# Attention, routing and two MLP layers on one core: another order for ScalarE's copies and the router's exp and ln

## The chip, the cores and the metric

The kernel runs on one core of a Trainium2 chip. A core has five engines that run their own instruction streams in order and meet at semaphores: TensorE (PE in the profile; PEld is its weight load), VectorE (DVE), ScalarE (ACT), GpSimd (POOL) and SyncE (SP). The metric is the device time of one execution in microseconds; less is better.

## The reference

`q`, `k`, `v` have 4 batches, 8 heads, 768 steps and a head width of 48; the token rows of width 384 go through two layers after the attention.

```python
k_n = k / (norm(k) + 1e-06)
for t in range(S):                                   # attention, a delta rule
    y[t]   = einsum('bhd,bhde->bhe', q[t], state)
    v_old  = einsum('bhde,bhd->bhe', state, k_n[t])
    state += beta[t] * einsum('bhd,bhe->bhde', k_n[t], v[t] - v_old)
x = y as 3072 x 384
noisy = x @ w_gate + log1p(exp(x @ w_noise)) * noise # routing, 8 experts, the best 2 of each token
out   = sum over the two of weight * (relu(x @ w1[e]) @ w2[e])
h     = out @ w_in                                   # second layer
final = (h * clip(h + 3, 0, 6) / 6) @ w_out
```

## The kernel before

The tokens are cut into 24 tiles of 128 rows (64 steps of two batches). A tile's delta rule is solved in blocks: Gram products of its rows, the inverse of a triangular matrix, and products with the state. Four tiles make a group. The loop of the attention takes two tiles, n and n+1, in each turn, for n = 0, 2, ..., 18; a turn whose n is a multiple of four is called a four turn here. The last four tiles are written out behind the loop.

The names that follow:

- `gram(a)` and `gram(a + 1)`, with a = n + 8, multiply the keys and queries of the tiles eight ahead (line 183) and put the copies of the result into a list `late`; `flush(k)` issues the first k copies of it, `flush()` all. The copies run on ScalarE: m0 and m1 fill `mq` (L187), o fills the off-diagonal block `goff` (L205), d0, d1 and d2 fill the diagonal pieces `gd` of the group (L199, then L202 twice). `gd` has one buffer. `masked` belongs to m.
- The inverse of a group runs on VectorE. Its head transposes `gd` (L276), its large products and reductions are L342 to L356, its tail transposes the result into `Xc` (L364) and `Yc` (L365). It is queued at the end of the turns n = 2, 6, 10 and 14 for the groups 2 to 5, and issued piece by piece as a credit that grows with TensorE's work allows (`run`).
- `merge1(n)` multiplies `goff` with `Xc` on TensorE (L389) and ScalarE copies the result to `y` (L392). `merge2(n)` multiplies `y` with `Yc` (L408), and ScalarE scales the result into `Xc` (L152, two pieces of 32 rows). `prep(n)` scales a part of `Xc` in place (L152, 128 rows). merge1(n+1) on TensorE waits for the last copy that wrote `Xc` ahead of it.
- `ks` (copied to `rz`, L431), `solve`, `update` (copied to `us`, L150) and `output` (copied to `x`, L150) are the products with the state.
- The router: `transposes` of a finished tile (L840) with the copy to `rt_xt` (L842), `logits` (L853, copied to `rt_ls`, L855). `route` gives stages for four tiles: exp on ScalarE (L880), ln on ScalarE (L883), a row of small VectorE operations (L888 and on, the noisy logits and the best two), counts, the rank on TensorE (L924 to L930, copied to `rt_rks` by ScalarE, L932; VectorE reads it into `rt_pos`, L934) and the moves of rows. One call of `step()` issues one stage; what it holds for VectorE is woven into the inverse's operations.
- `warm(m)` issues m matmuls of a zero tile on TensorE (L480).

The order of the instructions on each engine is that in which this code is written, except that VectorE's operations come out of the list `pend` by credit. Behind the attention the two layers follow, with TensorE busy nearly all the time.

Of the kernel before, what the change touches and what calls it, by code (L numbers as in the profile page):

```python
# [27 lines left out]
PQ = 1.3  # L28
P2 = 3
P3 = 1  # L30
P4 = 26
F = [0, 0, 2, 1, 0, 0, 0, 0]
FG = [2, 0, 1, 0, 0, 0, 0, 1]
FL = [1, 3, 3, 3, 1, 1, 0, 3]
# [9 lines left out]
KD = DM // 128  # L44
# [45 lines left out]
def emit_attention(ctx, tc, qk, k, v, beta, const, rt, moe):  # L90
# [77 lines left out]
    def load_beta(g):  # L168
        t = wk.tile([128, 32], F32, tag="beta", name="beta")
        nc.sync.dma_start(out=t, in_=beta[g])  # L170
        beta_t[g] = t

    def gram_tiles(n):
        g, j = divmod(n, 4)
        if j == 0:
            gd[g] = pr.tile([128, 32, 32], F32, tag="gd", name="gd", bufs=1)
        goff[n] = wk.tile([128, NH, 32], F32, tag="goff", name="goff", bufs=11)

    def products(n, gm, heads, lo, hi):
        for i, h in enumerate(heads):  # L180
            for b in range(2):
                m = mq[b][n % NM][st[b], :, h]
                nc.tensor.matmul(gm[tok[b], i, lo:hi], lhsT=m[:, 1, :], rhs=m[:, lo // 64:hi // 64, :],
                                 start=True, stop=True)

    def evict_m(n, gm, hs, b):
        nc.scalar.copy(out=mq[b][n % NM][tok[b], 0, hs, :], in_=gm[tok[b], :, 0:64])  # L187

    def masked(n):
        if n < 6:  # L190
            masks.append(n)
        else:
            mask(n)

    def evict_d(n, gm, hs, part):
        g, j = divmod(n, 4)
        d = gd[g][:, 8 * j + hs.start:8 * j + hs.stop, :]
        if part == 0:
            nc.scalar.copy(out=d, in_=gm[:, :, 64:96])  # L199
        else:  # L200
            p = slice(64 * part - 32, 64 * part)
            nc.scalar.copy(out=d[p], in_=gm[p, :, 96:128])  # L202

    def evict_o(n, gm, hs):
        nc.scalar.copy(out=goff[n][:, hs, :], in_=gm[:, :, 64:96])  # L205
# [25 lines left out]
    def gram(n):  # L231
        gram_tiles(n)
        gm = ps1.tile([128, NH, 128], F32, tag="gm", name="gm")
        hs = slice(0, NH)
        products(n, gm, range(NH), 0, 128)
        late.extend(lambda b=b: evict_m(n, gm, hs, b) for b in range(2))
        late.append(lambda: (masked(n), evict_o(n, gm, hs)))
        late.extend(lambda part=part: evict_d(n, gm, hs, part) for part in range(3))

    masks = []  # L240

    def mask(n):
        for b in range(2):
            m = mq[b][n % NM][tok[b], 0]
            nc.gpsimd.affine_select(out=m, in_=m, pattern=[[0, NH], [1, CH]], compare_op=ALU.is_gt,
                                    fill=0.0, base=0, channel_multiplier=-1)
# [133 lines left out]
    y1, xs = {}, {}  # L380
# [94 lines left out]
    def warm(m):  # L475
        if not m:
            return
        p = ps2.tile([128, 512], F32, tag="tp", name="wp")
        for _ in range(m):
            nc.tensor.matmul(p, lhsT=wz[:, 0:128], rhs=wz, start=True, stop=True)  # L480

    pend, late = [], []

    def flush(k=99):
        for _ in range(min(k, len(late))):
            late.pop(0)()
# [5 lines left out]
    def weave(ops, k=1):  # L492
        micro[0] += len(ops)

        def one(fn):
            fn()
            micro[0] -= 1

        ops = [(0.1, lambda fn=fn: one(fn)) for fn in ops]
        steps, last = pend[:-1], pend[-1:]  # L500
        pend[:] = []
        for it in steps:
            pend.append(it)
            pend.extend(ops[:k])
            ops = ops[k:]
        pend.extend(ops + last)

    def step(drain=False):
        if drain:
            while stages or micro[0]:  # L510
                while micro[0]:
                    pend.pop(0)[1]()
                if stages:
                    weave(stages.pop(0)() or [])
        elif stages and not micro[0]:
            weave(stages.pop(0)() or [], 2)
            run(0.0)

    def straight(k):
        for _ in range(k):  # L520
            for fn in stages.pop(0)() or []:
                fn()
# [4 lines left out]
    def run(t, drain=False):  # L527
        credit[0] = min(credit[0] + t, 4.0) if pend else 0.0
        while pend:
            c, fn = pend[0]  # L530
            if not drain and credit[0] < c:
                break
            pend.pop(0)
            credit[0] -= c
            fn()
        if drain:
            credit[0] = 0.0
# [6 lines left out]
    def live(fn, n, *args):  # L544
        if 0 <= n < NT:
            fn(n, *args)
            cur = pc[0] - LA
            if fn in beat:
                rt.beat = beat[fn](n)
                lives[0] += 1  # L550
            tok = rt.moves[0][0] if rt.moves else NT
            if tok < NT - 16 and fn in beat and lives[0] % 2 == 0 and cur >= tok // 4 * 4 + 8 or \
                    NT - 16 <= tok < NT - 12 and fn in beat and cur >= NT - 8 or \
                    NT - 12 <= tok < NT - 8 and cur >= NT - 6 and fn not in (load_v, load_k, load_qk, v_norm):
                rt.moves.pop(0)[1]()
                if tok >= NT - 12 and not rt.moves:
                    moe.snap_load()
            run((PACE if pc[0] < NT else PACE_L) * PE_US.get(fn.__name__, 0.0))
# [29 lines left out]
    for i in range(8, 16):  # L588
        n, hh = divmod(i, 2)
# [15 lines left out]
    ks(1)  # L605
    warm(P4)
    for i in range(2):
# [6 lines left out]
    for n in range(0, NT - 4, 2):  # L614
        a = n + LA
        four = n % 4 == 0
        pc[0] = a
        if not four and a // 4 + 1 < NG:
            load_beta(a // 4 + 1)
        for i in range(2):  # L620
            live(load_v, n + 4 + i)
            if n + 4 < NT:
                live(load_k, n + 2 + i)
        for i in range(2):
            if n + 2 + i > 3:
                live(v_norm, n + 2 + i)
        if n == NT - 6:
            moe.snapshot(pk, ps2)
        if n:
            warm(W0.get(n, W0[-(four + 1)]))  # L630
            live(merge1, n)
            live(prep, n)
            live(ks, n)
            rt.transposes(n - 2, xs.pop(n - 2))
            live(gram, a)
            live(prep, n + 1)
            if n != NT - 6:
                step()
            live(merge2, n)
            flush(2)  # L640
            live(ks, n + 1)
            live(merge1, n + 1)
            if n == NT - 6:
                straight(2)
            live(solve, n)
            live(merge2, n + 1)
            flush()
            rt.transposes(n - 1, xs.pop(n - 1))
            rt.logits(n - 2)
        else:  # L650
            live(solve, n)
            live(gram, a)
            flush()
        step()
        live(update, n)
        live(solve, n + 1)
        if n:
            rt.logits(n - 1)
            if four:
                step(True)  # L660
                stages += rt.route(n - 4, 4)
                if n == NT - 8:
                    straight(2)
        live(output, n)
        live(load_qk, a + 2)
        if n == NT - 8:
            straight(2)
        elif not four:
            step()
        live(gram, a + 1)  # L670
        live(update, n + 1)
        flush(2)
        live(output, n + 1)
        if n == NT - 6:
            rt.reserve()
            while rt.moves:
                rt.moves.pop(0)[1]()
                if not rt.moves:
                    moe.snap_load()
        flush()  # L680
        live(load_qk, a + 3)
        if n != NT - 8:
            step()
        if not four:
            run(0.0, True)
            if n == NT - 10:
                step()
            if n // 4 + 2 < NG:
                pend += inverse_ops(n // 4 + 2)
                run(2.3)  # L690
    step(True)
    n = NT - 4
# [76 lines left out]
class Router:  # L769
# [64 lines left out]
    def store(self, n, x):  # L834
        self.nc.sync.dma_start(out=self.xd[n * 128:(n + 1) * 128, :], in_=x)

    def transposes(self, n, x):
        tp = self.ps.tile([128, 4, 128], F32, tag="tp", name="tpx", bufs=2)
        for k in range(KD):
            self.nc.tensor.transpose(tp[:, k, :], x[:, k * 128:(k + 1) * 128], self.const["ident"])  # L840
        xt = self.wk.tile([128, KD, 128], F32, tag="rt_xt", name="rt_xt", bufs=2)
        self.nc.scalar.copy(out=xt, in_=tp[:, 0:KD, :])  # L842
        self.xt[n] = xt

    def logits(self, n):
        nc = self.nc
# [828 lines left out]
```

## Time and profile before

| | |
|---|---|
| three runs | 1187.56, 1191.43, 1191.59 us; median 1191.43 us |
| profiled execution | 1189.55 us, span 1187.8 us, mean granted clock of TensorE 0.955 |
| busy, share of the span | PE 96%, DVE 57%, ACT 43%, POOL 25% |
| 0 to 258.7 us, loop of the attention | PE busy 230.68 us, DVE 230.22, ACT 174.59; clock 0.87 |
| 258.7 to 298 us, last four tiles and routing | PE busy 32.51 us of 39.3; clock 0.67 |
| 298 to 1187.8 us, the two layers | PE busy 876.40 us of 889.8; clock 0.99 |

In the rows further down, a line of a timeline holds the start in us from the span's start, the duration in us, the engine, the kernel's line and operation, what it writes and reads, the number of instructions in a row, and in brackets the idle time before it with what ended it. A row of a table of stretches holds the busy time of each engine in the stretch.

### The profile page before, as it was taken

The numbers are of one execution on the slowest core, as the hardware profiler recorded it, in microseconds if no ns is written. First come the engines' busy times: TensorE is split into PE (matmuls) and PEld (weight loads), VectorE is DVE, ScalarE is ACT, GpSimd is POOL, SyncE is SP. The second block draws the span as 40 slices with busy tenths as digits, with TensorE's granted clock in tenths as the row PEclk, the third lists the DMA queues.
The fourth block names the chain that finished last, engine by engine and source line by source line (L and its number), as shares of the span: only waits on it lengthen the run. The fifth ranks groups of instructions, "written<-read, shape, count | busy, mean of one in ns | idle before, by whom it ended". The sixth has DMA issues, their size and how long they took to land. (4 is left out here: it accounts for less than half of the span.)

```text
span 1187.8 us, 25674 instructions
## 1 busy us (share of the span) xinstructions
PE 1139.6 (96%) x10578; PEld 1047.3 (88%) x10593; DVE 677.7 (57%) x1573; ACT 509.8 (43%) x1060; POOL 302.5 (25%) x370
## 2 busy tenths in 40 slices
PE   8899989878899999999999999999999999999998
PEld 5588878777699999999999999979989898989988
DVE  7999789885538676756565534444251614334250
ACT  5578767635514232323232324454251514334240
POOL 4542356562534223222223230132000000000000
PEclk9898977967799999999999999999999999999999
DMA  7642443424064464445343310732101020200000
GB/s 200 145 132 75 114 91 70 69 48 143 2 245 164 141 207 135 159 147 190 118 172 119 129 50 10 233 105 71 34 27 51 3 73 8 66 15 8 20 1 27
DMA packets 56220, 113.35 MB, mean 95 GB/s; under 512 B 9368, under 2 KB 37221, under 8 KB 55334
## 3 DMA queue, kind: packets, MB, share of 16 engines
q1 hardware_dynamic: 47142, 90.32, 25.5%
q0 software_dynamic: 8448, 19.70, 5.1%
q10 hardware_dynamic: 512, 1.67, 0.6%
q8 instruction: 84, 1.38, 0.5%
q14 instruction: 34, 0.28, 0.1%
HBM read 83.74 MB, written 26.08 MB: 92 GB/s over the span
## 5 line engine op out<-in xcount | busy, mean ns | idle before, releaser
L1224 PE MATMUL yp<-w2h,ht 128*128 128x384 f32 x832 | 221.2, 340 | 0.0
L1224 PE MATMUL yp<-w2l,ht 128*128 128x384 f32 x448 | 150.4, 336 | 0.0
L1224 PEld LDWEIGHTS yp<-w2h,ht 128*128 128x128 f32 x832 | 148.4, 188 | 0.3
L1014 POOL DMA_INDIRECT y<-ys,idp x56 | 64.9, 1159 | 303.2 <-DVE ys L1233 224.1
L1201 PE MATMUL hp<-xth,w1h 128*128 128x416 f32 (+2 forms) x384 | 137.9, 359 | 1.2 <-DVE xtl L1143 1.2
L1201 PE MATMUL hp<-xtl,w1h 128*128 128x416 f32 (+2 forms) x384 | 136.7, 356 | 0.0
L1201 PE MATMUL hp<-xth,w1l 128*128 128x416 f32 (+2 forms) x384 | 136.5, 355 | 0.0
L1564 PE MATMUL yp<-woh,gh 128*128 128x384 f32 x384 | 130.4, 340 | 0.0
L1564 PE MATMUL yp<-wol,gh 128*128 128x384 f32 x384 | 129.1, 336 | 0.0
L1564 PE MATMUL yp<-woh,gl 128*128 128x384 f32 x384 | 129.1, 336 | 0.0
L1204 ACT ACTIVATE ht<-hp 128x416 fp32r<-128x416 f32 (+2 forms) x128 | 66.3, 518 | 132.6 <-PE hp L1201 132.5
L1207 DVE SCALAR_TENSOR_TENSOR ht<-hp,ht 128x352 fp32r<-128x352 f32 (+3 forms) x192 | 79.3, 441 | 64.6 <-ACT ht L1204 64.2
L1532 PE MATMUL hp<-xh,wih 128*128 128x512 f32 x288 | 112.7, 391 | 2.6 <-DVE three L1518 2.6
L1532 PE MATMUL hp<-xh,wil 128*128 128x512 f32 x288 | 112.9, 392 | 0.0
L1532 PE MATMUL hp<-xl,wih 128*128 128x512 f32 x288 | 112.8, 392 | 0.0
L1541 DVE TENSOR_TENSOR gl<-r,gh 128x512 fp32r<-128x512 f32 x96 | 66.5, 693 | 79.6 <-ACT gh L1540 79.6
L1535 ACT ACTIVATE r<-hp,three 128x512 f32<-128x512 f32 x96 | 66.1, 688 | 89.7 <-PE hp L1532 87.2
L1537 DVE SCALAR_TENSOR_TENSOR r<-r,hp 128x512 f32<-128x512 f32 x96 | 65.4, 681 | 53.2 <-ACT r L1535 53.2
L1224 PEld LDWEIGHTS yp<-w2l,ht 128*128 128x128 f32 x448 | 84.1, 188 | 0.0
L1571 ACT ACTIVATE os<-yp 128x384 f32<-128x384 f32 x23 | 11.3, 491 | 152.8 <-PE yp L1564 152.8
L1201 PEld LDWEIGHTS hp<-xth,w1h 128*128 128x128 f32 x384 | 73.2, 191 | 3.9 <-DVE xtl L1143 1.6
L1201 PEld LDWEIGHTS hp<-xth,w1l 128*128 128x128 f32 x384 | 73.2, 191 | 2.1
(228 smaller groups left out, 2199.5 us busy)
## 6 DMA issues: line engine op xcount, KB each, us to landing
r<-in_moe_w_dram SPq DMA_DIRECT2D x16, 768.0 KB
r<-in_moe_w_dram SPq DMA_DIRECT2D x21, 512.0 KB
yg<-y SPq DMA_DIRECT2D x24, 384.0 KB
wd_r<-in_moe_w_in_dram SPq DMA_DIRECT2D x6, 1024.0 KB
wd_r<-in_moe_w_out_dram SPq DMA_DIRECT2D x8, 768.0 KB
mq<-in_qk_dram SPq DMA_DIRECT2D x28, 192.0 KB
v<-in_v_dram SPq DMA_DIRECT2D x24, 192.0 KB
xd<-x SPq DMA_DIRECT2D x24, 192.0 KB
```

The source lines that it names most:

```text
L1014: return nc.gpsimd.indirect_dma_start(out=y, out_offset=bass.IndirectOffsetOnAxis(ap=idx, axis=0), in_=src, in_offset=None, bounds_check=y ...
L1201: nc.tensor.matmul(p[:, 0:w], lhsT=a[:, k, fs], rhs=b[:, k, c], start=(i == 0), stop=(i == 3 * KD - 1))
L1204: nc.scalar.activation(out=h[:, c], in_=p[:, 0:w], func=ACTF.Relu)
L1207: nc.vector.scalar_tensor_tensor(out=h[:, rest(lo, hi)], in0=p[:, lo - c.start:hi - c.start], scalar=0.0, in1=h[:, lo:hi].bitcast(F32), op ...
L1224: nc.tensor.matmul(p[0:2 * m if pair else m, 0:DM], lhsT=a, rhs=b[:, f, :], start=f == i == 0, stop=f == FT - 1 and i == len(terms) - 1)
L1532: nc.tensor.matmul(p, lhsT=a[:, k, fs], rhs=b[:, k, :], start=(i == 0), stop=(i == 3 * KD - 1))
L1535: nc.scalar.activation(out=r, in_=p, func=ACTF.Relu, bias=three)
L1537: nc.vector.scalar_tensor_tensor(out=r, in0=r, scalar=6.0, in1=p, op0=ALU.min, op1=ALU.mult)
L1541: nc.vector.tensor_tensor(out=gl[:, f, :], in0=r, in1=gh[:, f, :].bitcast(F32), op=ALU.subtract)
L1564: nc.tensor.matmul(p[:, 0:DM], lhsT=a[:, f, c], rhs=b[:, f, :], start=(i == 0), stop=(i == 3 * FT2 - 1))
L1571: nc.scalar.mul(out=t, in_=p[:, 0:DM], mul=1.0 / 6.0)
```

## The change

Five things change.

1. Of the copies of a Gram the diagonal pieces d0, d1, d2 now come first, then o, then m0 and m1 with `masked`. For the first Gram of a turn one copy (d0) is issued ahead of ks(n+1) and the rest behind merge2(n+1). For the second Gram four copies (d0, d1, d2, o) are issued right behind it, ahead of `update`, and the two m copies behind `output`.
2. merge2(n) comes right behind the first Gram; its copies into `Xc` are issued ahead of the copy to `rt_xt`, which `transposes` now hands back instead of issuing it. prep(n+1) comes behind merge1(n+1).
3. The `step()` in the middle of the turn comes behind merge2(n).
4. At the end of the four turns n = 4, 8 and 12 a second `step()` follows the first: ln comes right behind exp. (The turn n = 16 has no step there.)
5. `P4`, the warming matmuls ahead of the first merge, goes from 26 to 32.

```diff
-P4 = 26
+P4 = 32
...
-        late.extend(lambda b=b: evict_m(n, gm, hs, b) for b in range(2))
-        late.append(lambda: (masked(n), evict_o(n, gm, hs)))
         late.extend(lambda part=part: evict_d(n, gm, hs, part) for part in range(3))
+        late.append(lambda: evict_o(n, gm, hs))
+        late.append(lambda: evict_m(n, gm, hs, 0))
+        late.append(lambda: (evict_m(n, gm, hs, 1), masked(n)))
...
-            rt.transposes(n - 2, xs.pop(n - 2))
+            copies = []
+            rt.transposes(n - 2, xs.pop(n - 2), copies)
             live(gram, a)
-            live(prep, n + 1)
+            live(merge2, n)
+            copies.pop()()
             if n != NT - 6:
                 step()
-            live(merge2, n)
-            flush(2)
+            flush(1)
             live(ks, n + 1)
             live(merge1, n + 1)
+            live(prep, n + 1)
...
         live(gram, a + 1)
+        flush(4)
         live(update, n + 1)
-        flush(2)
         live(output, n + 1)
...
         if n != NT - 8:
             step()
+            if n and four:
+                step()
...
-    def transposes(self, n, x):
+    def transposes(self, n, x, later=None):
...
-        self.nc.scalar.copy(out=xt, in_=tp[:, 0:KD, :])
         self.xt[n] = xt
+        copy = lambda: self.nc.scalar.copy(out=xt, in_=tp[:, 0:KD, :])
+        if later is None:
+            copy()
+        else:
+            later.append(copy)
```

ScalarE at the end of the turn n = 4, from the copies of `us` of the last update to the first merge copy of the next turn. Before:

```order
L150 COPY us_152<-sd 48x384
L150 COPY us_156<-sd 48x384
L187 COPY mq_132<-gm 64x512
L187 COPY mq_142<-gm 64x512
L150 COPY x<-y 128x384
L205 COPY goff<-gm 128x256
L199 COPY gd<-gm 128x256
L202 COPY gd<-gm 32x256 x2
L880 ACT_TABLE_LOAD
L880 ACTIVATE rt_t<-rt_ls 128x32
L392 COPY y_1963<-mg 128x256
```

and now:

```order
L199 COPY gd<-gm 128x256
L202 COPY gd<-gm 32x256 x2
L205 COPY goff<-gm 128x256
L150 COPY us_152<-sd 48x384
L150 COPY us_156<-sd 48x384
L150 COPY x<-y 128x384
L187 COPY mq_132<-gm 64x512
L187 COPY mq_142<-gm 64x512
L889 ACT_TABLE_LOAD
L889 ACTIVATE rt_t<-rt_ls 128x32
L892 ACT_TABLE_LOAD
L892 ACTIVATE rt_t<-rt_t 128x32
```

The diagonal pieces and `goff` moved ahead of `us`, the copies to `mq` behind `x`, and ln (L892 now) with its table load directly behind exp.

ScalarE at the start of the turn n = 6, up to the copies of the first Gram. Before:

```order
L392 COPY y_1963<-mg 128x256
L152 ACTIVATE Xc<-Xc,half 128x8x32
L431 ACTIVATE rz_157<-ks 128x384
L842 COPY rt_xt<-tpx 128x384
L152 ACTIVATE Xc<-Xc,half 128x8x32
L883 ACT_TABLE_LOAD
L883 ACTIVATE rt_t<-rt_t 128x32
L152 ACTIVATE Xc<-mg 32x8x32 x2
L187 COPY mq_133<-gm 64x512
L187 COPY mq_143<-gm 64x512
L431 ACTIVATE rz_158<-ks 128x384
L392 COPY y_2070<-mg 128x256
```

and now:

```order
L393 COPY y_1970<-mg 128x256
L152 ACTIVATE Xc<-Xc,half 128x8x32
L432 ACTIVATE rz_157<-ks 128x384
L152 ACTIVATE Xc<-mg 32x8x32 x2
L848 COPY rt_xt<-tpx 128x384
L199 COPY gd<-gm 128x256
L432 ACTIVATE rz_158<-ks 128x384
L393 COPY y_2076<-mg 128x256
L152 ACTIVATE Xc<-Xc,half 128x8x32
```

The two merge copies into `Xc` stood behind `rt_xt`, prep and the ln, and stand directly behind `rz` now; of the Gram's copies one stands ahead of the second `rz` instead of two.

VectorE in the second half of the inverse of group 2, where the router's first small operations are woven in. Before:

```order
L342 TENSOR_TENSOR big<-A,TT 128x256
L345 TENSOR_REDUCE tmp<-big 128x16x4 x2
L353 TENSOR_TENSOR big<-T,tmp 128x1024
L353 TENSOR_TENSOR A<-T,tmp 128x768
L888 TENSOR_SCALAR rt_t<-rt_t 128x32
L889 SCALAR_TENSOR_TENSOR rt_t<-rt_t 128x32
L356 TENSOR_REDUCE T<-big 128x4x16
```

and now:

```order
L343 TENSOR_TENSOR big<-A,TT 128x256
L897 TENSOR_SCALAR rt_t<-rt_t 128x32
L898 SCALAR_TENSOR_TENSOR rt_t<-rt_t 128x32
L346 TENSOR_REDUCE tmp<-big 128x16x4
L899 SCALAR_TENSOR_TENSOR rt_t<-rt_t 128x32
L900 RECIPROCAL rt_t<-rt_t 128x32
L346 TENSOR_REDUCE tmp<-big 128x16x4
```

The first router operation (it reads exp's result) and the second (it reads ln's) moved ahead of two reductions and two products.

## Rows read from the trace of the kernel before

**Rows 1.** Stretches: from:to us, length, busy us (xinstructions) of PE PEld DVE ACT POOL, PEclk, DMA, GB/s.
```profile
298.00:1187.80 889.80, 876.40 (x4721) 826.90 (x4721) 427.48 (x786) 317.28 (x578) 158.53 (x155) 0.99 0.28 91
```
**Rows 2.** Timeline of VectorE, 84 to 217 us: start, us, instruction, idle before.
```profile
84.23 1.99 DVE L276 STREAM_TRANSPOSE A<-gd 128x1024 f32<-128x1024 f32 x1 [1.65 <-ACT gd L202]
...
105.76 1.27 DVE L345 TENSOR_REDUCE tmp<-big 128x64 f32<-128x768 f32 x2
...
127.05 1.99 DVE L276 STREAM_TRANSPOSE A<-gd 128x1024 f32<-128x1024 f32 x1 [6.36 <-ACT gd L202]
...
149.09 0.41 DVE L342 TENSOR_TENSOR big<-A,TT 128x256 f32<-128x256 f32 x1
...
170.25 1.98 DVE L276 STREAM_TRANSPOSE A<-gd 128x1024 f32<-128x1024 f32 x1 [2.71 <-ACT gd L202]
...
216.05 0.23 DVE L934 TENSOR_TENSOR rt_pos<-rt_rks,ebase 128x32 f32<-128x32 f32 x1 [4.19 <-ACT rt_rks L932]
```
**Rows 3.** Timeline of TensorE, 44 to 260 us.
```profile
44.80 0.69 PE L389 MATMUL mg<-Xc,goff 32*32 32x32 f32 x32 [3.80 <-DVE Xc L364]
...
83.84 0.69 PE L389 MATMUL mg<-Xc,goff 32*32 32x32 f32 x32
...
95.22 0.53 PE L853 MATMUL lg<-wgn,rt_xt 128*64 128x16 f32 x12 [0.28 <-ACT rt_xt L842]
...
96.64 1.96 PE L183 MATMUL gm<-mq 64*64 64x128 f32 x32
...
100.32 0.82 PE L480 MATMUL wp<-wz 128*128 128x512 bf16 x2
101.07 0.69 PE L389 MATMUL mg<-Xc,goff 32*32 32x32 f32 x32
...
109.11 0.69 PE L389 MATMUL mg<-Xc,goff 32*32 32x32 f32 x32 [1.99 <-ACT Xc L152]
...
123.97 1.47 PE L480 MATMUL wp<-wz 128*128 128x512 bf16 x5
125.37 0.69 PE L389 MATMUL mg<-Xc,goff 32*32 32x32 f32 x32
...
177.89 0.38 PE L408 MATMUL mg<-y,Yc 32*32 32x32 f32 x12 [0.92 <-issue]
...
215.92 0.69 PE L389 MATMUL mg<-Xc,goff 32*32 32x32 f32 x32
...
258.76 1.06 PE L389 MATMUL mg<-Xc,goff 32*32 32x32 f32 x32 [5.12 <-DVE Xc L364]
```
**Rows 4.** Timeline of ScalarE, 93 to 109 us, turn n = 4 into n = 6.
```profile
93.51 0.38 ACT L199 COPY gd<-gm 128x256 f32<-128x256 f32 x1
...
99.50 0.96 ACT L150 COPY us<-sd 48x384 f32<-48x384 f32 x2 [1.84 <-PE sd L451]
100.36 1.18 ACT L187 COPY mq<-gm 64x512 f32<-64x512 f32 x2
...
102.63 0.74 ACT L202 COPY gd<-gm 32x256 f32<-32x256 f32 x2
103.39 1.28 ACT L880 ACT_TABLE_LOAD   x1
...
106.89 1.28 ACT L883 ACT_TABLE_LOAD   x1
...
108.32 0.74 ACT L152 ACTIVATE Xc<-mg 32x256 f32<-32x256 f32 x2
```
**Rows 5.** Stretches, as in rows 1, of four pieces of the loop.
```profile
45.40:56.50 11.10, 10.57 (x172) 7.79 (x168) 10.28 (x34) 4.10 (x10) 5.30 (x9) 0.54 0.46 110
83.80:101.10 17.30, 16.82 (x483) 14.93 (x483) 16.08 (x80) 12.71 (x33) 4.19 (x7) 1.00 0.43 116
109.10:119.40 10.30, 10.06 (x219) 9.24 (x219) 10.02 (x33) 7.51 (x19) 1.31 (x2) 0.59 0.08 23
177.90:187.00 9.10, 9.10 (x165) 8.62 (x167) 9.07 (x41) 5.21 (x14) 6.78 (x10) 0.62 0.08 26
```

## Prediction, made from this alone

> **What bounds the kernel now.** I read the stages first. From 298.00 us on TensorE is busy 876.40 of 889.80 us at a granted clock of 0.99 [rows 1]. No instruction changes place there, so the rest of the program is a fixed length, and what the attention stage saves or loses goes straight to the end.
>
> In the attention stage I read VectorE's timeline next. From 84 to 258 us it runs four inverses (groups 2 to 5) nearly without a pause; its four long waits are rows [rows 2]: three times the inverse's first transpose waits for the diagonal pieces `gd` (1.65, 6.36 and 2.71 us), once `rt_pos` waits for the rank copied by ScalarE (4.19 us). Together that is 14.9 us. Then TensorE's starts: at 258.76 us it has itself waited 5.12 us for the last inverse's `Xc` [rows 3]. So the attention stage ends on VectorE's chain, and a VectorE wait that goes is worth its length until something else is late.
>
> Why `gd` is late is in TensorE's and ScalarE's rows. A turn from merge1(4) to merge1(6) takes 101.07 − 83.84 = 17.23 us, the next one 125.37 − 101.07 = 24.30 us [rows 3]. In the second, merge1(7) waits 1.99 us for ScalarE's `Xc` at 109.11 us, because the copy stands behind the load of ln's table (106.89 to 108.32 us) [rows 4]; and from there to 119.40 us the granted clock is 0.59, where the shorter turn had 1.00 [rows 5]. (1.00 is 2.4 GHz, 0.50 the lower level of 1.2 GHz; 0.59 is mostly the lower.) Three more warming matmuls stand in the long turn, 1.47 − 0.82 = 0.65 us [rows 3]. That leaves 24.30 − 17.23 − 1.99 − 0.65 = 4.4 us for the low clock. The turns n = 10 and 14 follow the same pattern.
>
> **The change part by part.** All sums are made in the profiled run: 1189.55 us, of which the span is 1187.8; the median of the three runs, 1191.43, is 1.88 above it. Negative numbers are time saved.
>
> *Diagonal pieces first.* In the second Gram of a turn, d0, d1, d2 and o now stand straight behind the Gram. ScalarE is idle for 1.84 us before 99.50 us, and the Gram ends at 96.64 + 1.96 = 98.60 us [rows 3, 4]: they start there instead of at the turn's end, where d1, d2 ran from 102.63 to 103.37. `gd` is complete 1.1 us after the Gram (0.38 + 0.74) [rows 4], so over 3 us earlier within its turn. At 84.23 us that takes the whole wait: **−1.65**.
>
> *The price in the first Gram.* The flush ahead of `rt_xt` of tile n−1 loses d0 (0.38 us) and gains both m copies (1.18 us) [rows 4]. The logits' matmul behind that copy already waited 0.28 us at 95.22 [rows 3]; it now comes 0.8 us later, 0.7 in the turn n = 2. Behind it on TensorE stand the output's matmuls and the second Gram. Zero to 0.8 a turn; I take 0.8, for the existing wait shows no slack.
>
> *Exp and ln together.* The ln leaves the place in front of the `Xc` copy: the 1.99 us of TensorE in turns 6, 10 and 14 go, and with it what made the clock fall, 4.4 us. In its new place it stands ahead of the copy of y, which merge2(n) waits for: between 0 and 1.43 us (one load with its activation, 108.32 − 106.89 [rows 4]); I take 0.6, as the pieces ahead of it start earlier. A turn n = 6 thus is 17.23 + 0.65 + 0.8 + 0.6 = 19.3 us, a turn n = 4 18.0. Nothing of that is end time: it makes `gd` early.
>
> But the router's instructions behind the ln also move on VectorE. They stood behind the large products (where VectorE arrived after 109 us); now they stand in front of the row of 105.76 us [rows 2], and VectorE works in order, so the rest of the inverse queues behind them, and merge1(8) on TensorE behind that. VectorE gets there at 105.76 − 1.65 = 104.1. The table loads begin at 103.39 − 0.9 (pieces started at 98.60, not 99.50) + 0.7 + 0.8 (logits, turns 2 and 4) = 104.0; two loads with their activations take 2 × 1.43, so ln is ready at 106.9 [rows 3, 4]. **A new wait of +2.6** (bounds: 0, if ScalarE is as early as VectorE; 7, if the clock falls in turn 4, below). Sum so far +0.95.
>
> *Second head.* VectorE is free at 127.05 − 6.36 + 0.95 = 121.6 [rows 2]. merge1(6) starts at 101.07 + 1.5 = 102.6; its second Gram 96.64 − 83.84 = 12.8 later plus 0.8 and 0.6, ends 1.96 after, the pieces 1.1 after that [rows 3, 4]: 119.9. The wait is gone: **−6.36**, sum −5.4.
>
> *Second route.* Its router instructions now stand ahead of the row of 149.09 us [rows 2], reached at 149.1 − 5.4 = 143.7, with 0.2 for the ops ahead 143.9. merge1(8) starts at 102.6 + 19.3 = 121.9; ln is ready as far behind it as behind merge1(4), 106.9 − 84.5 = 22.4: 144.4 with rounding. **+0.5**, sum −4.9.
>
> *Third head and rank.* merge1(10) starts at 121.9 + 18.0 = 139.9, its `gd` is due 12.8 + 1.4 + 1.96 + 1.1 later at 157.2, VectorE at 170.25 − 2.71 − 4.9 = 162.6 [rows 2]: **−2.71**, sum −7.6. For the rank, VectorE arrives at 216.05 − 4.19 − 7.6 = 204.3. TensorE, free for merge1(12) at 159.2, now waits a little for VectorE's `Xc` (about 2.5 us ahead of 162.6) and starts near 160; with 18.0 + 19.3 us and one turn at low clock (4.4; after the wait of 3.80 at 44.80 us the clock is 0.54 [rows 3, 5]) its next pair starts near 202, and the rank's matmuls stand ahead of that. The third ln, 22.4 behind merge1(12), is there by 182.6, with the low clock by 187.0, and VectorE by about 187: no wait, but no margin in the second case. **−4.19**, sum **−11.8**.
>
> *The rest.* Six more warming matmuls before merge1(0), 0.65 / 3 = 0.22 us each, 1.3 us in all, lie in the 3.80 us in which TensorE waits for `Xc` [rows 3]: nothing, unless that gap shrinks below 1.3. The merged block's copies ahead of `rt_xt`, prep(n+1) behind y and rank behind merge2 change what stands next on TensorE, not how much. SyncE and GpSimd issue in the same order. The last inverse moves as a whole, and TensorE's 5.12 us behind it stay.
>
> Sum: 1189.55 − 11.8 = 1177.8; from the median, **1179.6 us**.
>
> **The rivals.**
>
> *A, no new wait for ln.* If TensorE is some 3 us earlier in the turns 2 and 4 than I have it (the extra warming matmuls keep the clock that falls to 0.54 from 45.40 to 56.50 [rows 5], 11.1 × 0.46 = 5.1 us), ln is ready when VectorE comes. All four waits go, nothing is given back: 1191.43 − 14.9 = 1176.5. Against it: 3.80 us less 1.3 still leaves a gap of 2.5.
>
> *B, a new gap lets the clock fall in the turns that ran at full speed.* The logits' wait grows to about 1 us; a gap of 0.92 at 177.89 [rows 3] was followed by a clock of 0.62 to 187.00 [rows 5]. That is 4.4 us in turn 4, perhaps in turn 8 too. Then the first ln comes 4.4 later (wait 7.0), the head's waits still go, and the sum is −7.4; with turn 8, −3. Time 1184 to 1188.4, about 1186. Against it: the same row's 0.28 left the clock at 1.00.
>
> *C, slower.* The clock falls in all six turns from 4 to 14, and TensorE becomes the bound. It starts at 84.5; three pairs of 18.0 + 19.3 with 4.4 in each turn put merge1(16) at 84.5 + 111.9 + 26.4 = 222.8, against 215.92 now [rows 3]: +6.9, 1198. It decides from the point at which a pair of turns is longer than VectorE's part of it, some 43 us; with one low turn in a pair it is 41.7 and does not.
>
> *D, the gain is handed back or does not come.* What follows 258 us may hang on something that does not shift, or ScalarE may be as late as before: 1191.
>
> *E, the table loads cost twice what they show.* Each of the two loads followed by a pause as long as itself would make the block 2 × (1.43 + 1.28) = 5.4 us, both waits for ln 2.5 us longer, −6.8: 1184.6. The rows show no pause: the load of 1.28 us from 106.89 and its activation are done at 108.32 [rows 4]. The Trainium skill, page "ScalarE: Activation LUTs", section "What ACT_TABLE_LOAD costs", gives about 1283 ns for the load and about 1380 ns for a drain, 2.66 us for each switch. The trace agrees with the load and shows no drain.
>
> **How the numbers follow.** My sum 0.47; A 0.18; B 0.18; C 0.06; D 0.08; E 0.03. The time is that of the sum. The range goes from A's end in the profiled run, 1189.55 − 14.9 = 1174.7, to B's, 1188.4, both widened a little, 1174 to 1188.5; C and D lie outside, 0.14, and a little of the others. Half a per cent is 5.96 us, about what a measurement of this kernel can tell from no change: faster is below 1185.5, slower above 1197.4. Faster holds the sum, A, E and some half of B: 0.77; the rest of B and D, and the nearer misses, are same, 0.17; slower is C, 0.06.
>
> **What would show it.** In the profile after, VectorE's waits for `gd` and for the rank must be gone, and a new one of about 2.6 us must stand at the router's first instructions in the inverse that begins at 84 us, 0.5 in the next, with ScalarE's ln as releaser. TensorE's 1.99 us for `Xc` must be gone, and the clock in the stretch that was 109 to 119 us near 1. TensorE should wait for VectorE's `Xc` at merge1(12) and merge1(16). The logits' wait should be near 1 us with the clock still up behind it. Wrong it would be if `gd` waits stay, if the new wait is 5 us or more, or if TensorE's turns from n = 4 on run at a low clock.

## The result and the profile after

The changed kernel takes 1177.70 us (median of 20 runs), the kernel before 1189.29 us in as many; the ratio is 0.9908, 95% interval [0.9888, 0.9927]. By the medians that is 11.6 us faster; the forecast was 11.8 us, 1179.6. The ratio leaves out two of the changed kernel's runs that count as slow (1188.92 and 1185.28 us). The profiled execution took 1176.90 us against 1189.55, a span of 1175.2 against 1187.8.

The head of its page:

```profile
span 1175.2 us, 25700 instructions
...
PE 1124.4 (96%) x10599; PEld 1031.7 (88%) x10599; DVE 678.8 (58%) x1573; ACT 510.4 (43%) x1060; POOL 300.6 (26%) x370
```

VectorE's timeline of the changed kernel, the lines that answer to [rows 2], with the first wait for ln and the last transposition:

```profile
82.56 1.84 DVE L277 STREAM_TRANSPOSE A<-gd 128x1024 f32<-128x1024 f32 x1
...
107.84 0.37 DVE L898 SCALAR_TENSOR_TENSOR rt_t<-rt_t 128x32 f32<-128x32 f32 x1 [0.54 <-ACT rt_t L892]
...
122.72 1.88 DVE L277 STREAM_TRANSPOSE A<-gd 128x1024 f32<-128x1024 f32 x1
...
162.34 1.84 DVE L277 STREAM_TRANSPOSE A<-gd 128x1024 f32<-128x1024 f32 x1
...
202.76 0.14 DVE L943 TENSOR_TENSOR rt_pos<-rt_rks,ebase 128x32 f32<-128x32 f32 x1
...
243.09 1.90 DVE L365 STREAM_TRANSPOSE Xc<-T 128x1024 f32<-128x1024 f32 x1
```

None of the three heads waits any more, nor does the rank; one wait of 0.54 us for ln has come. The three heads come 1.7, 4.3 and 7.9 us earlier than in [rows 2], the rank 13.3.

TensorE's timeline, to be read against [rows 3]:

```profile
97.34 0.53 PE L862 MATMUL lg<-wgn,rt_xt 128*64 128x16 f32 x12 [1.16 <-ACT rt_xt L848]
...
103.19 0.69 PE L390 MATMUL mg<-Xc,goff 32*32 32x32 f32 x32
...
108.26 0.69 PE L409 MATMUL mg<-y,Yc 32*32 32x32 f32 x32 [0.94 <-ACT y L393]
109.95 0.69 PE L390 MATMUL mg<-Xc,goff 32*32 32x32 f32 x32
...
122.87 0.69 PE L390 MATMUL mg<-Xc,goff 32*32 32x32 f32 x32
...
162.50 0.69 PE L390 MATMUL mg<-Xc,goff 32*32 32x32 f32 x32
...
202.06 0.69 PE L390 MATMUL mg<-Xc,goff 32*32 32x32 f32 x32
...
245.04 1.06 PE L390 MATMUL mg<-Xc,goff 32*32 32x32 f32 x32 [7.35 <-DVE Xc L365]
...
285.03 0.79 PE L1210 MATMUL hp<-xth,w1h 128*128 128x512 f32 x1 [1.16 <-DVE xtl L1152]
```

and the row of before that answers to the last one, the first product of the layers:

```profile
297.92 0.79 PE L1201 MATMUL hp<-xth,w1h 128*128 128x512 f32 x1 [1.16 <-DVE xtl L1143]
```

The 1.99 us for `Xc` are gone. The waits of about 1 us for `rt_xt` and for y have taken their place. At the last group's start TensorE waits 7.35 us for VectorE instead of 5.12. Of the 13.7 us gained at that point 12.9 reach the layers.

The turns n = 6, 8, 10, 12 and 14 as stretches (columns as in rows 1):

```profile
103.19:122.87 19.68, 17.70 (x486) 15.32 (x485) 18.69 (x43) 18.01 (x43) 6.91 (x8) 1.00 0.38 108
122.87:141.11 18.24, 16.96 (x487) 15.09 (x487) 17.49 (x82) 13.90 (x37) 8.42 (x15) 1.00 0.44 112
141.11:162.50 21.39, 19.07 (x485) 16.65 (x484) 20.74 (x49) 18.20 (x44) 13.08 (x15) 0.92 0.48 97
162.50:181.10 18.60, 17.15 (x487) 15.17 (x486) 17.91 (x77) 13.80 (x37) 11.09 (x19) 1.00 0.51 108
181.10:202.06 20.96, 18.06 (x491) 15.62 (x490) 20.41 (x53) 19.16 (x46) 14.38 (x18) 1.00 0.39 89
```

The turn n = 6 takes 19.68 us instead of 24.30, at a clock of 1.00; the forecast said 19.3, and 18.0 for a four turn, which takes 18.24 and 18.60. The turns n = 10 and 14 are longer than that, 21.39 and 20.96 us.

### The profile page after: what moved, and what is told of

The parts are those of the page before. It is cut to its first block, busy times and chain, and to the rows that moved or that the text cites. A ratio compares the mean times of both kernels' runs of the same rounds, so it can differ in the third digit from the quotient of the medians.

```text
span 1175.2 us, 25700 instructions
## 1 busy us (share of the span) xinstructions
PE 1124.4 (96%) x10599; PEld 1031.7 (88%) x10599; DVE 678.8 (58%) x1573; ACT 510.4 (43%) x1060; POOL 300.6 (26%) x370
```

## The experiments

Two theories stood at the start. Theory 1: TensorE's turns set the loop in the kernel before, and what they lose is the wait for `Xc` with the low clock behind it. Theory 2: the early diagonal pieces carry the gain. The first three kernels add one part each to the kernel before, with its 26 warming matmuls; the fourth takes one part out of the changed kernel. Ratios are to the kernel before on the same chip.

**ln_only.** The second step alone, in the kernel before.

```diff
         if n != NT - 8:
             step()
+            if n and four:
+                step()
```

> The kernel before with one part of the change: a second step at the end of the four turns, so that ln stands behind exp and no longer in front of the merge copies into Xc. Theory 1 (in the kernel before TensorE's turns set the loop from 84 to 216 us and VectorE only waits for them; the 1.99 us wait and the low clock behind it, 6.4 us in each of three turns, are the loss): the three waits of TensorE for Xc go, the clock stays at 1.00 in the turns n = 6, 10, 14, VectorE's waits for gd at the second and third head and for the rank go, the 1.65 us at the first head stays, and the time falls by 11 to 13 us, as much as with the whole change. Theory 2 (the order of the diagonal pieces carries the gain): no more than 6 us.

Measured: 1183.62 us, ratio 0.9946 [0.9916, 0.9976], some 6 us. TensorE's timeline at the turn n = 6 and the stretch behind it:

```profile
106.89 0.69 PE L408 MATMUL mg<-y,Yc 32*32 32x32 f32 x32 [1.52 <-ACT y L392]
```
```profile
106.89:117.20 10.31, 10.31 (x229) 9.54 (x231) 10.17 (x32) 8.61 (x22) 2.75 (x3) 0.54 0.26 72
```

The 1.99 us for `Xc` went as expected, but a wait of 1.52 us for y came, 1.6 us in the turns 10 and 14, and the clock fell behind each of the three as before: 0.54. So the part is worth 6 us and not 11 to 13: theory 1 was right about the wait and wrong that the clock would stay up with it. The time alone would also fit theory 2, which said no more than 6 us; the next kernel decides between the two.

**diag_only.** The order of the Gram's copies alone.

```diff
-        late.extend(lambda b=b: evict_m(n, gm, hs, b) for b in range(2))
-        late.append(lambda: (masked(n), evict_o(n, gm, hs)))
         late.extend(lambda part=part: evict_d(n, gm, hs, part) for part in range(3))
+        late.append(lambda: evict_o(n, gm, hs))
+        late.append(lambda: evict_m(n, gm, hs, 0))
+        late.append(lambda: (evict_m(n, gm, hs, 1), masked(n)))
...
-            flush(2)
+            flush(1)
             live(ks, n + 1)
...
         live(gram, a + 1)
+        flush(4)
         live(update, n + 1)
-        flush(2)
```

> The kernel before with the new order of the Gram's copies alone (diagonal pieces first, four of them right behind the second Gram). Theory 1: gd comes over 3 us earlier and the 1.65 us at the first head goes, but TensorE's turns keep the 1.99 us and the low clock and get 0.8 us longer by the logits' wait, and the rank is not earlier: time between 0 and 4 us longer than before, none of the 11 us. Theory 2: 5 us or more are saved.

Measured: 1189.16 us, ratio 1.0002 [0.9975, 1.0029]. In its trace `gd` is waited for once, 1.26 us, where [rows 2] has 10.7 in all; but `Xc` still comes late for TensorE, and VectorE now waits at the rank:

```profile
110.69 0.69 PE L390 MATMUL mg<-Xc,goff 32*32 32x32 f32 x32 [1.45 <-ACT Xc L152]
```
```profile
217.56 0.47 DVE L935 TENSOR_TENSOR rt_pos<-rt_rks,ebase 128x32 f32<-128x32 f32 x1 [5.38 <-ACT rt_rks L933]
```

The rank comes from TensorE at the end of the turn n = 14, and TensorE is no earlier there. 9 us of head waits were taken away and returned further down, as a longer chain and a longer wait. Theory 2 has fallen: alone, the early diagonal pieces save nothing.

**merge_only.** merge2's copies ahead of `rt_xt`, prep behind the second merge, the middle step behind merge2.

```diff
-            rt.transposes(n - 2, xs.pop(n - 2))
+            copies = []
+            rt.transposes(n - 2, xs.pop(n - 2), copies)
             live(gram, a)
-            live(prep, n + 1)
+            live(merge2, n)
+            copies.pop()()
             if n != NT - 6:
                 step()
-            live(merge2, n)
             flush(2)
             live(ks, n + 1)
             live(merge1, n + 1)
+            live(prep, n + 1)
```

> The kernel before with merge2's copies ahead of the copy to rt_xt, prep of the second tile behind the second merge, and the middle step behind merge2; Gram copies and ln's step stay. Theory 1: ln now stands behind the Xc copies, so the 1.99 us of TensorE go here too, without the second step; y of the second tile comes about 1.3 us late instead, too short a gap for the clock to fall: 8 to 13 us saved. If it is ln's place next to exp that matters, the wait for y brings the clock down again and no more than 4 us are saved.

Measured: 1183.59 us, ratio 0.9968 [0.9942, 0.9995], 4 us where theory 1 said 8 to 13. The wait for `Xc` is gone; that for the second tile's y is 2.05 us where 1.3 was expected:

```profile
114.31 0.69 PE L408 MATMUL mg<-y,Yc 32*32 32x32 f32 x32 [2.05 <-ACT y L392]
```
```profile
114.30:124.80 10.50, 9.93 (x257) 8.38 (x257) 9.00 (x28) 8.36 (x22) 0.73 (x2) 1.00 0.21 60
192.20:202.40 10.20, 10.20 (x177) 9.53 (x179) 9.96 (x18) 6.38 (x17) 8.73 (x11) 0.52 0.08 21
```

Behind the wait at 114 us the clock stayed at 1.00, behind the same wait of 2.04 us at 192 us it fell to 0.52; behind the third, 2.04 us at 152 us, it was 0.84 to 163 us. A wait of this length may bring the clock down or not.

**no_extra_step.** The changed kernel without the second step.

```diff
-            if n and four:
-                step()
```

> The changed kernel without the second step, so that ln stands in the middle of the turns n = 6, 10, 14 behind the copy to rt_xt. Theory 1 (either of the two reorderings takes ln off the path): within 2 us of the changed kernel, VectorE's 0.54 us wait for ln gone, TensorE's waits of 1 us for the first y gone and one of about 1 us for the second y in their place. Rival (both are needed): 5 us or more slower than the changed kernel.

Measured: 1184.62 us, ratio 0.9977 [0.9949, 1.0004], which doesn't overlap the changed kernel's [0.9888, 0.9927]. So the second step is needed in the changed kernel, as the rival says. Whether merge2's place is needed beside it isn't shown: no run takes that alone out of the changed kernel. In its trace there is a wait of 1.11 us for the second y and one of 1.34 us for `rt_xt` within 5 us of each other (at 110.29 and 115.07 us); in the changed kernel these waits lie 8 us apart (108.26 and 116.37 us). That this is what costs the time is argued, not shown.

**after_again, xt_first_again, no_diag, p26.** The changed kernel once more, and three edits of it, on one chip.

```diff
 xt_first (both runs):
             live(merge2, n + 1)
-            flush()
+            flush(3)
             rt.transposes(n - 1, xs.pop(n - 1))
+            flush()
 no_diag: the three edits of diag_only, undone
 p26:
-P4 = 32
+P4 = 26
```

> The changed kernel once more, as the measure for the three kernels beside it and because the last four ran on another chip, where the kernel before took 1207.6 us. Expected: a ratio to the kernel before of 0.988 to 0.993 on whichever chip this is.

> The changed kernel with the copy to rt_xt of tile n-1 ahead of goff and the two mq copies. On the other chip it was at 0.989 of the kernel before, with VectorE waiting 5.7 us for gd and 5.6 us for the rank in its trace, so there TensorE's turns were the longer of the two. If TensorE bounds the changed kernel too, this one is 2 to 6 us faster than it in this call; if VectorE does, within 2 us, and TensorE waits longer for Xc at the group starts.

> The changed kernel with the old order of the Gram's copies (m0, m1, o, then the diagonal pieces). gd comes about 3 us later: the first head waits 1.7 us again, the second about 1.4, the third about 1.3, while the logits' waits on TensorE fall from 1 to 0.3 us. Theory 1: VectorE's waits for gd come back in part, 1 to 5 us slower than the changed kernel; the diagonal pieces, worth nothing alone, are worth this once ln is out of the way. Rival (the order of the pieces is worth nothing here either): within 1 us of the changed kernel.

> The changed kernel with 26 warming matmuls ahead of the first merge instead of 32. The wait of TensorE at merge1(0) grows from 2.5 to 3.8 us, merge1(0) starts at the same time, the clock falls after it as with 32: within 1 us of the changed kernel. If the six matmuls shorten the low clock behind that wait, up to 4 us slower.

| | median us | ratio to before |
|---|---|---|
| changed kernel | 1177.34 | 0.9906 [0.9874, 0.9938] |
| xt_first_again | 1181.91 | 0.9945 [0.9923, 0.9967] |
| no_diag | 1179.40 | 0.9915 [0.9886, 0.9945] |
| p26 | 1183.81 | 0.9960 [0.9933, 0.9987] |

In xt_first_again and xt_first the edit puts the copy to `rt_xt` ahead of the two `mq` copies only; `goff` stays ahead of it (111.85 and 112.12 us in the trace), unlike what their expectations say.

The second profile of the changed kernel shows how its own time is made. TensorE's wait, the stretch behind it, and VectorE's next head:

```profile
106.83 0.69 PE L409 MATMUL mg<-y,Yc 32*32 32x32 f32 x32 [0.93 <-ACT y L393]
```
```profile
107.50:121.00 13.50, 13.50 (x269) 12.65 (x269) 13.26 (x35) 9.59 (x25) 2.21 (x3) 0.56 0.17 51
```
```profile
124.17 1.97 DVE L277 STREAM_TRANSPOSE A<-gd 128x1024 f32<-128x1024 f32 x1 [2.13 <-ACT gd L202]
```

Same program, a wait of 0.93 us where the first profile had 0.94, and this time the clock fell: the turn took 24.29 us instead of 19.68, `gd` came 2.13 us late, and the last `Xc` at 245.28 us instead of 243.09. In this kernel VectorE's chain and TensorE's turns lie so close that a turn longer by 4.6 us costs VectorE 2. The profiled run is only 0.4 us longer all the same, since its layers took 1.7 us less.

*xt_first_again*: in the loop from 90 to 200 us no logits' wait for `rt_xt` is left, merge1(12) waits 2.10 us for VectorE's `Xc`,

```profile
159.10 1.06 PE L390 MATMUL mg<-Xc,goff 32*32 32x32 f32 x32 [2.10 <-DVE Xc L365]
```

and the last `Xc` is at 243.30 us, as in the changed kernel. In this execution TensorE's turns are shorter and nothing follows: VectorE's chain bounds it. But it took 1176.57 us, 5.3 less than the kernel's median, and the median is 4.6 us above the changed kernel's; the intervals overlap, so this is no gain and perhaps a loss that the trace doesn't show. On the other chip the same kernel's trace has VectorE waiting 5.72 us for `gd` and 5.58 for the rank, so which of the two engines bounds it differs from profile to profile.

*no_diag*: 2 us from the changed kernel, not told apart. In its trace the first head doesn't wait, the second waits 1.01 us for `gd`, and at the third the wait is back,

```profile
167.14 1.97 DVE L276 STREAM_TRANSPOSE A<-gd 128x1024 f32<-128x1024 f32 x1 [4.95 <-ACT gd L202]
```

and the profiled run is 2.7 us longer than the changed kernel's beside it. The waits speak for theory 1; the times don't decide, for the means lie 1.1 us apart with a 95% interval of about -3 to 5 us.

*p26*: the intervals overlap by a hair (0.9933 to 0.9938), but that is no test of the difference. Its 12 times have a mean of 1183.3 us, the 8 of the changed kernel beside it 1177.5: 5.8 us apart, with a 95% interval of about 1.6 to 10.0 worked out from these times. So "within 1 us" is wrong, and the six warming matmuls are worth about 6 us; "up to 4 us slower" lies inside the interval. Seen from the kernel before, p26, which has the four other parts of the change, is 5.3 us faster, and the rest of the gain needs the matmuls.

How they earn it isn't shown. The mean granted clock is 0.963 over p26's runs and 0.970 over the changed kernel's, so more time goes at the low level. In p26's trace merge1(0) waits 3.81 us instead of 2.52 and starts at 44.78 us, and little differs until 162 us: the three heads come 2.2, 5.6 and 7.6 us earlier than in [rows 2], without a wait. Then the turns n = 12 and 14 run at a clock of 0.78 and 0.73 and the rank is late by 4.12 us:

```profile
162.78:185.57 22.79, 21.63 (x487) 19.45 (x487) 21.97 (x86) 14.07 (x37) 11.45 (x20) 0.78 0.37 89
185.57:211.18 25.61, 23.62 (x491) 20.99 (x490) 18.46 (x44) 19.33 (x46) 14.54 (x20) 0.73 0.30 72
```
```profile
211.07 0.47 DVE L943 TENSOR_TENSOR rt_pos<-rt_rks,ebase 128x32 f32<-128x32 f32 x1 [4.12 <-ACT rt_rks L941]
```

That is 118 us and more behind the edit, and one profile can't say that the edit put it there. What the profiles do show is a pattern at the edit's place, in the stretch from 45.40 to 56.50 us. In all fourteen profiles its clock is 0.50 to 0.69 behind the ten waits of 2.51 us and more (0.54 in [rows 5], behind 3.80 us) and 1.00 behind the four of up to 1.83 us, as here:

```profile
45.40:56.50 11.10, 10.72 (x291) 8.91 (x284) 10.28 (x28) 7.87 (x20) 6.65 (x11) 1.00 0.55 122
```
```profile
45.40:56.50 11.10, 10.72 (x298) 9.21 (x298) 10.45 (x35) 8.14 (x20) 6.41 (x10) 1.00 0.55 140
```

The first is no_diag, with a wait of 1.59 us, the second xt_first_again, with 0.52. Six more warming matmuls shorten the wait by 1.3 us, so more executions may stay up. But in these two TensorE then waits 2.73 and 2.94 us for `Xc` at merge1(4), so they don't show that the time won there lasts. The cause of the 6 us stays open.

**vnorm_twice, vnorm_late, xt_first, xt_vnorm.** They test why VectorE reached the router's operations 2 us later than forecast, 106.5 instead of 104.1. The changed kernel's trace, VectorE and GpSimd at the first head:

```profile
86.63 0.86 DVE L298 TENSOR_TENSOR sm<-sm 128x32 f32<-128x32 f32 x1
87.53 0.86 DVE L299 SCALAR_TENSOR_TENSOR sm<-sm 128x32 f32<-128x32 f32 x1
88.43 0.87 DVE L297 SCALAR_TENSOR_TENSOR sm<-sm 128x32 f32<-128x32 f32 x1
89.33 0.19 DVE L298 TENSOR_TENSOR sm<-sm 128x32 f32<-128x32 f32 x1
```
```profile
85.69 3.56 POOL L418 TENSOR_TENSOR us<-v,rows 64x384 f32<-64x384 f32 x4
```

The same kind of operation takes 0.86 us while GpSimd's four products run (3.56 / 4 = 0.89 us each) and 0.19 behind them. In the kernel before the four ran from 83.29 us, under VectorE's wait and its transpose.

```diff
 vnorm_twice:
             if n + 2 + i > 3:
+                if n and four:
+                    v_norm(n + 2 + i, True)
                 live(v_norm, n + 2 + i)
...
-    def v_norm(n):
+    def v_norm(n, keep=False):
...
-        t = vt.pop(n)
+        t = vt[n] if keep else vt.pop(n)
 vnorm_late (xt_vnorm: with the edit of xt_first):
-            if n + 2 + i > 3:
+            if n + 2 + i > 3 and not (n and four):
                 live(v_norm, n + 2 + i)
...
+        if n and four:
+            live(v_norm, n + 2)
         live(gram, a + 1)
         flush(4)
         live(update, n + 1)
+        if n and four:
+            live(v_norm, n + 3)
         live(output, n + 1)
```

> The changed kernel, in which GpSimd scales v twice in the turns n = 4, 8, 12 and 16 (the same four products once more, about 0.9 us each, result unchanged), right under the small operations at an inverse's head. Theory C (a small VectorE operation that meets a GpSimd operation waits for it: in the changed kernel's first inverse four operations of 0.19 us take 0.86 us while GpSimd's four products run): four to five more operations of each of the four inverses are lengthened by about 0.67 us, VectorE's chain gets 8 to 13 us longer, and the time with it, 8 to 13 us above the changed kernel. Rival (the long operations have another cause and GpSimd is off the path): within 2 us of the changed kernel.

> The changed kernel with GpSimd's scaling of v in the turns n = 4, 8, 12, 16 moved from the turn's start to its last third, under the inverse's large products. Theory C: the four operations of 0.86 us at the inverse's head fall to 0.19; VectorE's chain is 2 to 3 us shorter for each inverse, but gd comes only 1.8 us ahead of VectorE at the second head, so TensorE's turns end the gain at once: 1 to 4 us saved against the changed kernel. Rival: no change of these operations.

> The changed kernel with the copy to rt_xt of tile n-1 ahead of goff and the two mq copies of the first Gram. The logits' waits of 0.9 to 1.3 us in each turn go (below 0.4 us), TensorE's turns are about 1 us shorter. If VectorE's chain bounds the changed kernel, TensorE only waits longer for Xc at merge1(12), merge1(16) and merge1(20) and the time stays within 2 us; if TensorE still bounds it, 4 to 6 us are saved.

> Both of these edits. If VectorE's chain and TensorE's turns are two nearly equal bounds in the changed kernel, the two together save more than the sum of each alone: 4 to 8 us against the changed kernel, 1170 to 1174 us. If one alone is the bound, the two together save what the better of them saves.

These four ran on another chip, where the kernel before took 1207.57 us and the changed kernel was not run beside them; so their times can't be set against it. Ratios to before: vnorm_twice 0.9937 [0.9912, 0.9963], vnorm_late 0.9963 [0.9934, 0.9993], xt_first 0.9890 [0.9840, 0.9939], xt_vnorm 1.0011 [0.9977, 1.0045]. The expected differences to the changed kernel are not tested by them; the traces are. In vnorm_twice seven operations in a row are long, with GpSimd's eight products over them:

```profile
86.97 0.87 DVE L297 SCALAR_TENSOR_TENSOR sm<-sm 128x32 f32<-128x32 f32 x1
...
92.37 0.87 DVE L301 TENSOR_TENSOR sm<-sm 128x32 f32<-128x32 f32 x1
93.27 0.18 DVE L302 TENSOR_SCALAR sm<-sm 128x32 f32<-128x32 f32 x1
```
```profile
86.01 7.18 POOL L418 TENSOR_TENSOR us<-v,rows 64x384 f32<-64x384 f32 x8
```

From head to `Xc` the three inverses that begin near 82, 126 and 170 us take 38.6, 38.1 and 41.3 us; in xt_first on the same chip 34.8, 36.0 and 38.6. That is 2.1 to 3.7 us for four more products, against 4 x 0.68 = 2.7. It is a rough measure, for xt_first has another edit and the same spans differ by up to 2.2 us between the two profiles of the changed kernel; the operations' own durations are what bears theory C out. Its 8 to 13 us of time are not tested. In vnorm_late L297 to L299 at the first head all take 0.19 us. Whether that gains time can't be told on this chip; TensorE now waits for the scaled v:

```profile
PE ks L430 <- POOL us L418: 7.4, 3, 3.2
```

(a line of the table of waits: total us, times, longest.) xt_vnorm has the same 7.4 us, and no more can be said of the two edits together. The Trainium skill, page "SBUF — State Buffer", section "Who interferes with whom", calls the pair of ports that VectorE and GpSimd share an exclusive lock, and says that a VectorE instruction with two SBUF inputs contends with a GpSimd instruction that reads SBUF. The trace agrees: L297 to L299 read two SBUF inputs each, and beside GpSimd's products of 0.89 us they take 0.86 to 0.87 us instead of 0.19.

## Why the prediction was right, point by point

**The bound and the sum.** VectorE's four waits went as forecast, 14.9 us [rows 2], and the end moved with VectorE's chain. Step by step, as cumulative time against [rows 2], forecast and measured: first head -1.65 and -1.7; second -5.4 and -4.3; third -7.6 and -7.9; rank -11.8 and -13.3. The last `Xc` is 13.7 us earlier, the layers 12.9, the profiled run 12.65, the medians 11.6. These steps are those of one profile: in the second one of the changed kernel they are -0.2, -2.9, -5.6 and -10.6, with a wait of 2.13 us at the second head, and the layers come 10.8 us earlier. The forecast's steps are right in kind, and in size to within 1.5 us in the first profile and 2.5 in the second.

**Two terms of the first inverse were mis-sized and nearly cancelled.** The wait for ln was put at 2.6 us and is 0.54. (106.9 less 104.1 is 2.8; the 2.6 holds only with 0.2 us for the operations ahead, which the prediction names at the second route alone.) ScalarE was later than forecast (ln ready at 107.8, not 106.9), but VectorE was later still: four operations lengthened by 0.67 us beside GpSimd's products make 2.7 us. From its first head to the second the inverse took 3.2 us longer (1.6 in the second profile), without the wait, than in the kernel before; the prediction took VectorE's own work as fixed and had no term for what else moves under it. 0.54 + 3.2 = 3.7 us against 2.6: that is the 1.1 us missing at the second head. In the later inverses it ran the other way: without waits the stretches between [rows 2] were 0.9, 1.2 and 0.4 us shorter, and the wait of 0.5 us for the second ln did not come. GpSimd's products beside the small operations don't explain the first two: behind the second head four of these operations are long in both kernels, behind the third none before and one now. Why the stretches got shorter is open. So the sum was close partly by luck.

**Which part earns it.** The prediction booked the diagonal pieces with the first 1.65 us and ln with making `gd` early, and didn't say that the first is worth nothing without the second. diag_only shows it: TensorE's turns were the bound, so VectorE's waits were the sign and not the cause. ln's place and merge2's place are worth some 6 and 4 us alone, and these don't add up: all four reorderings with the old 26 warming matmuls (p26) are worth 5.3 us, no more than ln's place by itself. Taken out of the changed kernel, the second step costs about 7 us by the medians, the six matmuls about 6, the diagonal pieces 2, not told from nothing.

**The turns.** The logits' wait (forecast near 1 us, measured 0.9 to 1.3) and the turn lengths (19.3 and 18.0; 19.68 and 18.24) were right, but for the turns n = 10 and 14 of the first profile (21.39 and 20.96 us) and n = 6 and 14 of the second (24.29 and 22.94). The wait for y, 0.6 of a bound of 1.43, is 0.9 to 1.0. That TensorE would wait for `Xc` at merge1(12) and merge1(16) was wrong in the changed kernel's first profile, where the turn n = 10 ran at 0.92 and TensorE came at 162.50 without a wait.

**The rivals.** B, the clock falling behind a new gap of about 1 us, is real, but in another turn: the second profile of the changed kernel has it in n = 6, at 4.6 us, and not in a four turn, so that ln came in time and 2 us were lost at the end instead of B's 4 to 9. C, the slower side, needs a fall in all six turns; the two profiles of the changed kernel show one and two. D came in a small part: 0.8 us between the last `Xc` and the layers. A's time, 1176.5, is as near as the sum's, but its mechanism didn't come: all four waits went, yet ln wasn't early through TensorE, for merge1(4) starts at 85.17 us and not 3 us ahead of the forecast's 84.5, and VectorE's own work took 0.67 us more over the four stretches. E did not come: two table loads with their activations take 104.75 to 107.81 us, 3.1 us with no pause.

**The six warming matmuls** were booked at nothing, because TensorE waits there anyway. This term failed: p26 puts them at about 6 us. And the −11.8 us were booked on the four reorderings alone, which in p26 are worth 5.3 us (1.5 to 8.0 by its interval). In p26's profile the three head steps come out as forecast, and the step that fails is the rank: its −4.19 rested on one turn at the low clock in the pair n = 12 and 14, 41.7 us, and the pair took 48.4. One term too large by about 6 us and one too small by as much made the time come out right, and that is luck. What the matmuls would earn alone in the kernel before was not run.

## What to carry to other kernels

Before an engine's waits are booked as gain, ask which engine makes it wait and whether that engine gets earlier: taking away 9 us of waits alone gave nothing here. A part that is booked at nothing because its engine waits anyway deserves a run without it: here it was half of the gain. When work moves in time on one engine, look at what another engine does beside it: 0.19 us operations became 0.86 us because GpSimd's products now ran beside them. Where a wait near 1 us sits in a loop of an otherwise busy TensorE, take at least two profiles, for the clock may fall behind it in one and not in the other.

## What the runs showed of the hardware

- A gap's length alone doesn't tell whether TensorE's clock falls to 1.2 GHz: behind 0.94 us it stayed at 1.00 in one profile of the changed kernel, behind 0.93 us it was 0.56 in another; behind 2.05 us it stayed, behind 2.04 us in the same profile (merge_only) it was 0.52.
- A VectorE operation on 32 columns takes 0.19 us alone and 0.86 to 0.87 us when it meets a GpSimd product of 0.89 us, in a row as long as such products last.
- The attention stage was not equally fast on the two chips: the kernel before took 1188 to 1189 us on three occasions and 1207.6 us on the other chip. The kernel xt_first was profiled on both: its layers began at 284.4 us and at 308.0 us, and took 890.5 and 894.4 us.
